# A linear-attention and token-mixer kernel: one hand-given order for all engines, q and k cast by GpSimd's DMAs, states summed on TensorE

## The chip, the core and the metric

The kernel runs on one core of a Trainium2 chip. The core has a matrix engine (TensorE, called PE in the profile, with its weight loads shown apart as PEld), a vector engine (VectorE, DVE), a scalar engine (ScalarE, ACT), a general engine (GpSimd, POOL) and an engine that here only issues DMAs (SyncE, SP). Each of them works through its own instructions in order and waits on semaphores that the others raise. Data comes from and goes to HBM through 16 DMA engines, and any of SP, ACT and POOL may issue a transfer. PE writes to PSUM, which has 8 banks; DVE and ACT bring results from there to SBUF.

The metric is the device time of one execution in microseconds. Three runs of the kernel before gave 156.98 us in the median (156.47 to 158.2).

## The reference

All of q, k and v are [4 batches, 8 heads, 768 positions, 64], in float32. A block-wise linear attention with a decay per head is followed by a mixer over positions:

```python
for b in range(nb):                                  # blocks of 64 positions
    intra = einsum('bhic,bhjc->bhij', qb, kb) * Dmask
    intra = einsum('bhij,bhjd->bhid', intra, vb)
    inter = einsum('bhid,bhde->bhie', qb * lam_pow, kv_state)
    out[:, :, sl] = intra + inter
    kv_state = lam_block * kv_state + einsum('bhsd,bhse->bhde', kb * rev_pow, vb)
x = out.transpose(0, 2, 1, 3).reshape(B, S, H * D)   # [4, 768, 512]
wq, wk = x @ w_q, x @ w_k                            # [4, 768, 64] each
W_tok = einsum('bsd,btd->bst', wq, wk) / sqrt(64)
mixed = einsum('bst,btd->bsd', W_tok, x)
return maximum(mixed, 0) @ w_out                     # [4, 768, 512]
```

Since the decay is a power of the distance, the kernels fold `lam**i` into q and `lam**-j` into v. Then the mask is plain causal, and a state is a plain sum of k-times-v products over all earlier positions.

## The kernel before

The work is cut into 16 pairs: pair n is batch n // 4 and two heads. A pair has six chunks of 128 positions. Its two heads stand in partitions 0 to 63 and 64 to 127.

For each pair, `load` (line 59) issues three DMAs of 384 KB on SP, for q, k and v in float32 (tiles fq, fk, fv). `prepare` then has these steps. POOL casts q and k to bfloat16 (qn line 157, kn line 159) and multiplies v by the decay (vn line 161). PE turns q and k chunk by chunk (trq line 169, trk line 174; six 128-by-128 transposes each). DVE multiplies the turned q by the decay while it brings it from PSUM (qT line 171), and ACT copies the turned k (kT line 176). PE makes the five chunk products of k and v for both heads (dps line 181, ten matmuls), and one DVE scan (gs line 190) adds them up to prefix sums, which are the states.

`attend` works in two halves of three chunks: scores (sc line 212), state times q (oa line 228), mask and cast on DVE (pr line 240), v times masked scores into the same PSUM tile (oa line 246), and the copy to the feature-major result xT on ACT (line 254). `flip` turns xT back to position-major (xp line 260, xnat line 261).

When a batch's four pairs are done, `mixer` runs for it as a generator whose parts are put between the pairs of the next batch: projections (pq line 271, qkT line 278), the turned key side (pk line 281, wkn line 285), py (line 288) and Y (line 292), the mixed result (pm line 298, rmT line 305), and six output tiles (po line 312 on PE, osb line 320 on ACT, and a 256 KB DMA on SP, line 321). The last batch's mixer stands alone at the end.

The order in which the engines get this is set by a scheduler: the code gives the data flow, and the scheduler fills each engine's queue. SP's queue holds the loads and the output DMAs in one line, and each entry can wait. All PSUM tiles come from one pool of 8 banks; staging has 9 buffers for each of fq, fk and fv.

Of the kernel before, what the change touches and what calls it, by code (L numbers as in the profile page):

```python
# [16 lines left out]
CH = 128  # L17
# [4 lines left out]
HALF = 3 * CH  # L22


@with_exitstack
def kernel(
# [28 lines left out]
    def load(b, kk):  # L55
        st = {}
        for nm, src in (("q", q), ("k", k), ("v", v)):
            t = stage.tile([128, 2, NCH, D], F32, tag="f" + nm, name="f" + nm)
            nc.sync.dma_start(  # L59
                out=t,  # L60
                in_=src[b, 2 * kk : 2 * kk + 2].rearrange("h (c p) d -> p h c d", p=128),
            )
            st[nm] = t
        return st
# [4 lines left out]
    staged = {0: load(*pairs[0]), 1: load(*pairs[1])}  # L69


    ident = consts.tile([128, 128], BF16, name="ident")
    make_identity(nc, ident)
    ET = consts.tile([128, S], F32, name="ET")
    nc.gpsimd.iota(
        ET,
        pattern=[[1, S]],
        base=1,
        channel_multiplier=0,
        allow_small_or_imprecise_dtypes=True,  # L80
    )
# [8 lines left out]
    maskc = consts.tile([128, 3, CH], BF16, name="maskc")  # L90
    nc.gpsimd.memset(maskc, 1.0)
    nc.gpsimd.affine_select(
        out=maskc,
        in_=maskc,
        compare_op=ALU.is_ge,
        fill=0.0,
        base=0,
        pattern=[[0, 3], [1, CH]],
        channel_multiplier=-1,
    )  # L100
    coef = consts.tile([128, D, NCH - 1], F32, name="coef")
    nc.vector.memset(coef, 1.0)
    nc.vector.memset(coef[:, :, 0:1], 0.0)

    nc.scalar.preload_act_table_set("natural_log_exp_and_others")
    lnl = consts.tile([128, H], F32, name="lnl")
    nc.scalar.activation(out=lnl, in_=lam_all, func=ACT.Ln)
    lnv = lnl.rearrange("p (k l) -> p k l", l=2)
    lncol = consts.tile([128, NP], F32, name="lncol")
    for hl in range(2):  # L110
        nc.vector.tensor_copy(
            out=lncol[hl * 64 : hl * 64 + 64, :], in_=lnv[hl * 64 : hl * 64 + 64, :, hl]
        )
# [6 lines left out]
    )  # L120
    DvI = consts.tile([128, H, NCH], F32, name="DvI")
# [7 lines left out]
    W = {}  # L129

    def load_weights():
        wqk_f = consts.tile([128, 4, 2 * DHY], F32, name="wqk_f")
# [6 lines left out]
        wqk = consts.tile([128, 4, 2 * DHY], BF16, name="wqk")  # L139
# [4 lines left out]
        wo_f = consts.tile([128, 4, HD], F32, name="wo_f")  # L144
        nc.sync.dma_start(out=wo_f, in_=moe_w_out.rearrange("(kt p) j -> p kt j", p=128))
        wo = consts.tile([128, 4, HD], BF16, name="wo")
        nc.gpsimd.tensor_copy(out=wo, in_=wo_f)
        W["qk"], W["o"] = wqk, wo


    xT, xnat = {}, {}

    def prepare(n):
        b, kk = pairs[n]
        f = staged.pop(n)
        qn = nat.tile([128, NCH, 2, D], BF16, tag="qn", name="qn")
        nc.gpsimd.tensor_copy(out=qn, in_=f["q"].rearrange("p h c d -> p c h d"))  # L157
        kn = nat.tile([128, NCH, 2, D], BF16, tag="kn", name="kn")
        nc.gpsimd.tensor_copy(out=kn, in_=f["k"].rearrange("p h c d -> p c h d"))  # L159
# [3 lines left out]
            in0=f["v"],  # L163
# [3 lines left out]
        trq = pst([128, S], BF16, "trq")  # L167
# [32 lines left out]
    def attend(n, L):  # L200
# [5 lines left out]
        for a in range(2):  # L206
# [15 lines left out]
            for cc in range(3):  # L222
                c = 3 * a + cc
                if c == 0:
                    continue
# [38 lines left out]
    def mixer(b):  # L264
# [44 lines left out]
        for t in range(NCH):  # L309
# [12 lines left out]
            if t % 3 == 2:  # L322
                yield
# [52 lines left out]
```

## Time and profile before

| what | value |
|---|---|
| median of three runs | 156.98 us (156.47 to 158.2) |
| the profiled execution's own time | 157.66 us |
| its span, first to last instruction | 155.9 us |
| PE busy / weight loads / DVE / ACT / POOL | 126.3 / 71.5 / 61.8 / 64.7 / 55.5 us |
| read from HBM / written to it | 20.19 MB / 6.29 MB |
| instructions | 3005 |

The span is the profile's clock: views of the trace count from its start. The profiled execution took 1.76 us more than its span, and was 0.68 us above the median.

A group row names a line of the code, an engine, an operation and its tiles, a count, and then the busy time and the mean of one. Rows of the timeline and of the chain start with the start time and the length in us. Matmuls overlap in PE's pipeline, so a matmul's mean is its latency; how many get through in a time is read from the chain, where each piece counts only until the next one starts.

### The profile page before, as it was taken

The numbers are of one execution on the slowest core, as the hardware profiler recorded it, in microseconds if no ns is written. First come the engines' busy times: TensorE is split into PE (matmuls) and PEld (weight loads), VectorE is DVE, ScalarE is ACT, GpSimd is POOL, SyncE is SP. The second block draws the span as 40 slices with busy tenths as digits, with TensorE's granted clock in tenths as the row PEclk, the third lists the DMA queues.
The fourth block names the chain that finished last, engine by engine and source line by source line (L and its number), as shares of the span: only waits on it lengthen the run. The fifth ranks groups of instructions, "written<-read, shape, count | busy, mean of one in ns | idle before, by whom it ended". The sixth has DMA issues, their size and how long they took to land.

```text
span 155.9 us, 3005 instructions
## 1 busy us (share of the span) xinstructions
PE 126.3 (81%) x1200; PEld 71.5 (46%) x1200; DVE 61.8 (40%) x121; ACT 64.7 (41%) x123; POOL 55.5 (36%) x61
## 2 busy tenths in 40 slices
PE   0234788988899899999498999998298999997890
PEld 0133455646563556465343656554153655543340
DVE  1113536364572286381350458182060647322000
ACT  3831023313122358536222356635204385453881
POOL 5364655475456633003444563004345500000000
PEclk9999999999999999999955699999957999999999
DMA  3999999999999940179999990299999100423055
GB/s 72 222 222 219 218 219 240 293 206 220 209 218 214 226 76 0 69 202 234 307 232 202 228 153 4 81 252 256 279 203 226 24 0 0 169 105 135 0 189 214
DMA packets 79694, 26.67 MB, mean 171 GB/s; under 512 B 76097, under 2 KB 76097, under 8 KB 79681
## 3 DMA queue, kind: packets, MB, share of 16 engines
q1 hardware_dynamic: 79680, 26.49, 79.3%
q8 instruction: 9, 0.15, 0.4%
q14 instruction: 5, 0.03, 0.1%
HBM read 20.19 MB, written 6.29 MB: 170 GB/s over the span
## 4 chain that ended last, share of the span: by engine, by line
PE 47%; SPq 19%; DMA 15%; DVE 6%; issue 5%; POOL 3%; ACT 3%; DVEq 0%; POOLq 0%; ACTq 0%
SPq L59 17%; DMA fv<-in_v_dram 13%; PE po L312 10%; PE oa L246 7%; PE pq L271 6%; PE py L288 5%; PE pm L298 4%; PE oa L228 4%; POOL vn L161 3%; PE xp L260 3%; PE dps L181 3%; DVE pr L240 2%; PE sc L212 2%; PE trq L169 2%; DMA out_dram<-osb 1%
## 5 line engine op out<-in xcount | busy, mean ns | idle before, releaser
L254 ACT CAST xT<-oa 128x384 bf16<-128x384 f32 x32 | 15.3, 479 | 45.9 <-PE oa L246 45.7
L240 DVE TENSOR_TENSOR pr<-sc,maskc 128x384 bf16<-128x384 f32 x64 | 30.8, 544 | 0.0
L161 POOL TENSOR_TENSOR vn<-fv,DvI 128x768 bf16<-128x768 f32 x16 | 23.5, 1472 | 19.7 <-DMA fv<-in_v_dram 14.3
L312 PE MATMUL po<-wo,rmT 128*128 128x512 bf16 x96 | 25.2, 382 | 0.0
L157 POOL CAST qn<-fq 128x768 bf16<-128x768 f32 x16 | 13.2, 823 | 32.2 <-DMA fq<-in_q_dram 31.8
L246 PE MATMUL oa<-pr,vn 128*64 128x128 bf16 x192 | 20.8, 263 | 1.3 <-DVE pr L240 1.3
L261 DVE COPY xnat<-xp 128x768 bf16<-128x768 bf16 x16 | 8.9, 555 | 29.5 <-PE xp L260 29.5
L190 DVE TENSOR_TENSOR_SCAN gs<-coef,dps 128x320 bf16<-128x320 f32 x16 | 13.1, 821 | 17.7 <-PE dps L181 17.4
L176 ACT COPY kT<-trk 128x768 bf16<-128x768 bf16 x16 | 12.9, 807 | 16.8 <-PE trk L174 16.8
L246 PEld LDWEIGHTS <-vn 128*64 128x64 bf16 x192 | 10.6, 124 | 19.1 <-issue 18.1
L228 PE MATMUL oa<-qT,gs 64*64 64x128 bf16 x160 | 18.6, 285 | 0.0
L159 POOL CAST kn<-fk 128x768 bf16<-128x768 f32 x16 | 13.2, 827 | 14.3 <-DMA fk<-in_k_dram 14.3
L169 PE MATMUL trq<-ident,qn 128*128 128x128 bf16 x96 | 10.9, 259 | 7.1 <-POOL qn L157 7.1
L181 PE MATMUL dps<-vn,kn 128*64 128x64 bf16 x160 | 9.4, 286 | 8.3 <-POOL vn L161 8.2
L305 ACT ACTIVATE rmT<-pm 128x384 bf16<-128x384 f32 x32 | 13.4, 510 | 5.4 <-PE pm L298 5.4
L171 DVE TENSOR_TENSOR qT<-trq,dq 128x768 bf16<-128x768 bf16 x16 | 8.9, 554 | 16.6 <-PE trq L169 14.1
L320 ACT COPY osb<-po 128x512 f32<-128x512 f32 x24 | 14.0, 599 | 3.3 <-PE po L312 1.7
L228 PEld LDWEIGHTS <-gs 64*64 64x64 bf16 x160 | 10.6, 158 | 7.5 <-issue 4.7
L260 PE MATMUL xp<-ident,xT 128*128 128x128 bf16 x96 | 10.9, 247 | 2.9 <-ACT xT L254 2.8
L212 PE MATMUL sc<-qT,kT 64*128 64x128 bf16 x192 | 12.9, 250 | 0.0
L174 PE MATMUL trk<-ident,kn 128*128 128x128 bf16 x96 | 10.2, 257 | 3.0 <-POOL kn L159 3.0
L181 PEld LDWEIGHTS <-kn 128*64 128x64 bf16 x160 | 6.9, 149 | 10.3 <-issue 9.2
(37 smaller groups left out, 91.3 us busy)
## 6 DMA issues: line engine op xcount, KB each, us to landing
fq<-in_q_dram SPq DMA_DIRECT2D x16, 384.0 KB, 6.2
fk<-in_k_dram SPq DMA_DIRECT2D x16, 384.0 KB, 6.2
fv<-in_v_dram SPq DMA_DIRECT2D x16, 384.0 KB, 6.3
out_dram<-osb SPq DMA_DIRECT2D x24, 256.0 KB, 2.2
wo_f<-in_moe_w_out_dram SPq DMA_DIRECT2D x1, 1024.0 KB, 7.0
wqk_f<-in_moe_w_q_dram SPq DMA_DIRECT2D x1, 128.0 KB, 6.1
wqk_f<-in_moe_w_k_dram SPq DMA_DIRECT2D x1, 128.0 KB, 4.8
lam_all<-in_lam_dram SPq DMA_DIRECT2D x1, 4.0 KB, 3.4
```

What stands on the lines that cost most here:

```text
L59: nc.sync.dma_start(out=t, in_=src[b, 2 * kk : 2 * kk + 2].rearrange("h (c p) d -> p h c d", p=128),)
L161: nc.gpsimd.tensor_tensor(out=vn, in0=f["v"], in1=DvI[:, 2 * kk : 2 * kk + 2, :].unsqueeze(3).to_broadcast([128, 2, NCH, D]), op=ALU.mult,)
L169: nc.tensor.transpose(trq[:, c * CH : (c + 1) * CH], qn[:, c, :, :], ident)
L181: nc.tensor.matmul(dps[hl * 64 : hl * 64 + 64, :, c], kn[:, c, hl, :], vn[:, hl, c, :], start=True, stop=True, skip_group_check=True,)
L212: nc.tensor.matmul(sc[hl][:, cc, :], kT[r, c * CH : (c + 1) * CH], qT[r, c * CH : (c + 1) * CH], start=True, stop=True, skip_group_check=True,
L228: nc.tensor.matmul(oa[r, cc, :], gs[r, :, c - 1], qT[r, c * CH : (c + 1) * CH], start=first[hl], stop=False, skip_group_check=True,)
L240: nc.vector.tensor_tensor(out=t, in0=sc[hl], in1=maskc, op=ALU.mult)
L246: nc.tensor.matmul(oa[r, cc, :], vn[:, hl, c, :], pr[hl][:, cc, :], start=False, stop=(cc == 2), skip_group_check=True,)
L254: nc.scalar.copy(out=xT[b][:, kk, a * HALF : (a + 1) * HALF], in_=oa)
L260: nc.tensor.transpose(xp[:, t, :], xT[b][:, kk, t * CH : (t + 1) * CH], ident)
L312: nc.tensor.matmul(po, rmT[:, kt, t * CH : (t + 1) * CH], wo[:, kt, :], start=(kt == 0), stop=(kt == 3),)
L320: nc.scalar.copy(out=osb, in_=po)
```

## The change

The tiles and the mathematics stay; what each engine gets, and when, is rewritten.

- **Order.** A manual schedule is switched on: each engine gets its instructions in the order of the code. The code is cut into small functions (`turn`, `states`, `scores`, `inter`, `values`, `flip`, and the mixer's parts) that a loop over the pairs puts in a row. In iteration n PE does the scores of n, transposes of n+1, the flip of n-1, pieces of an earlier batch's mixer, then state times q, v times scores, and the states of n+1.
- **Loads.** v stays on SP in float32. q and k are issued by POOL, with a cast to bfloat16 in the DMA, and no POOL cast is left for them. They run seven pairs ahead (`AHEAD`). q is read two positions at a time (rows of 512 bytes, 768 of them in place of 1536); the order of positions within qT, the scores and the mask changes accordingly, and the copy to xT puts them back.
- **Transposes.** They are made head by head, 24 of 128 by 64 per pair in place of 12 of 128 by 128.
- **States.** Each chunk's product is written to all later states at once, as a matmul whose moving operand repeats v (m times 64 columns, m from 5 to 1) and which adds up in PSUM. A DVE copy takes the place of the scan, and the states lie in one piece for each chunk.
- **Mixer.** Its parts come later: four of a batch's six output tiles are made two batches on; the last batch's end holds four output tiles of the batch before.

The core of the diff:

```diff
+    ctx.enter_context(tc.manual_schedule())
-            nc.sync.dma_start(
-                out=t,
-                in_=src[b, 2 * kk : 2 * kk + 2].rearrange("h (c p) d -> p h c d", p=128),
-            )
+    def load_q(n):
+        t = stage.tile([128, 2, 3, 2 * D], BF16, tag="fq", name="fq")
+        nc.gpsimd.dma_start(
+            out=t,
+            in_=q[b, 2 * kk : 2 * kk + 2].rearrange("h (a p r) d -> p h a (r d)", p=128, r=2),
+        )
+    def load_kv(n):
+        t = stage.tile([128, 2, NCH, D], F32, tag="fv", name="fv")
+        nc.sync.dma_start(
+            out=t, in_=v[b, 2 * kk : 2 * kk + 2].rearrange("h (c p) d -> p h c d", p=128)
+        )
+        t = stage.tile([128, 2, NCH, D], BF16, tag="fk", name="fk")
+        nc.gpsimd.dma_start(
+            out=t, in_=k[b, 2 * kk : 2 * kk + 2].rearrange("h (c p) d -> p h c d", p=128)
+        )
...
-        nc.gpsimd.tensor_copy(out=qn, in_=f["q"].rearrange("p h c d -> p c h d"))
-        nc.gpsimd.tensor_copy(out=kn, in_=f["k"].rearrange("p h c d -> p c h d"))
...
-            nc.tensor.transpose(trq[:, c * CH : (c + 1) * CH], qn[:, c, :, :], ident)
+                    nc.tensor.transpose(
+                        trq[hl * 64 : hl * 64 + 64, a, r, :],
+                        fq[:, hl, a, r * D : (r + 1) * D],
+                        ident,
+                    )
...
-                    vn[:, hl, c, :],
-                    start=True,
-                    stop=True,
+                    vn[:, hl, c, :].unsqueeze(1).to_broadcast([128, m, D]),
+                    start=(c == 0),
+                    stop=(c == NCH - 2),
...
-        nc.vector.tensor_tensor_scan(
+        nc.vector.tensor_copy(out=gs, in_=dps)
...
     for n in range(N):
+        b, kk = pairs[n]
+        if n + AHEAD < N:
+            load_kv(n + AHEAD)
+            load_q(n + AHEAD)
         if n + 2 < N:
-            staged[n + 2] = load(*pairs[n + 2])
+            cast(n + 2)
         if n == 1:
-            load_weights()
+            cast_weights()
+
+        scores(n)
+        if b >= 1 and kk == 1:
+            mix_pk(b - 1)
+        if b >= 1 and kk == 2:
+            mix_pm(b - 1, 0)
+        if b >= 1 and kk == 3:
+            mix_pm(b - 1, 1)
         if n + 1 < N:
-            ready[n + 1] = prepare(n + 1)
-        attend(n, ready.pop(n))
...
+            turn(n + 1)
+        if n >= 1:
+            flip(n - 1)
+        if b >= 1 and kk == 0:
+            mix_pq(b - 1)
+        if b >= 1 and kk == 1:
+            mix_py(b - 1)
+        done = {0: [(2, 2)], 1: [(2, 3)], 2: [(2, 4), (2, 5)], 3: [(1, 0), (1, 1)]}[kk]
+        for back, t in done:
+            if b >= back:
+                mix_po(b - back, t)
+
+        inter(n)
+        values(n)
+        if n + 1 < N:
+            states(n + 1)
+    bl = B - 1
+    flip(N - 1)
+    mix_pq(bl)
+    mix_po(bl - 1, 2)
+    mix_pk(bl)
+    mix_po(bl - 1, 3)
+    mix_py(bl)
+    mix_po(bl - 1, 4)
+    mix_po(bl - 1, 5)
+    mix_pm(bl, 0)
+    mix_pm(bl, 1)
+    for t in range(NCH):
+        mix_po(bl, t)
```

What this does to the queues, at three places. On SP, in the middle of the program before (rows of its queue, in order; a row that stands for several in a row has their count at its end), the loads of a pair stand behind three output DMAs:

```order
L59 DMA fk<-in_k_dram 128x12x64
L59 DMA fv<-in_v_dram 128x12x64
L321 DMA out_dram<-osb 128x512 x3
L59 DMA fq<-in_q_dram 128x12x64
L59 DMA fk<-in_k_dram 128x12x64
L59 DMA fv<-in_v_dram 128x12x64
L321 DMA out_dram<-osb 128x512 x3
```

SP's whole queue after it:

```order
L85 DMA lam_all<-in_lam_dram 128x8
L74 DMA fv<-in_v_dram 128x12x64 x3
L152 DMA wqk_f<-in_moe_w_q_dram 128x4x64
L155 DMA wqk_f<-in_moe_w_k_dram 128x4x64
L158 DMA wo_f<-in_moe_w_out_dram 128x4x512
L74 DMA fv<-in_v_dram 128x12x64 x12
L382 DMA out_dram<-osb 128x512 x2
L74 DMA fv<-in_v_dram 128x12x64
L382 DMA out_dram<-osb 128x512 x22
```

Of the loads only v's last one still stands behind output DMAs. On POOL before, three operations of one pair follow one another:

```order
L157 CAST qn<-fq 128x768
L159 CAST kn<-fk 128x768
L161 TENSOR_TENSOR vn<-fv,DvI 128x768
L157 CAST qn<-fq 128x768
L159 CAST kn<-fk 128x768
```

On POOL after, around the loop's first two iterations, with the semaphores that each waits for (DMASW are those of POOL's own DMAs, DMAHW those of SP's; POOL has eight DMASW and uses them in turn):

```order
L79 DMA fk<-in_k_dram 128x12x64 [waits DMASW6_49]
L65 DMA fq<-in_q_dram 128x6x128 [waits DMASW7_49]
L176 TENSOR_TENSOR vn<-fv,DvI 128x768 [waits DMAHW3_49]
L79 DMA fk<-in_k_dram 128x12x64 [waits DMASW0_49]
L65 DMA fq<-in_q_dram 128x6x128 [waits DMASW1_49]
L176 TENSOR_TENSOR vn<-fv,DvI 128x768 [waits DMAHW7_49,PE_49,Pool_49]
```

A q or k load now waits until the eighth DMA before it on POOL has landed, and the multiplication vn(n+2) stands behind the loads of pair n+7, which wait for those of pair n+3. On DVE, in a later batch, the program before has, from one pair's copies to the next pair's scan:

```order
L261 COPY xnat<-xp 128x6x128
L171 TENSOR_TENSOR qT<-trq,dq_126 128x768
L190 SCALAR_TENSOR_TENSOR gs<-coef,dps 128x320
L240 TENSOR_TENSOR pr<-sc_1140,maskc 128x384
L240 TENSOR_TENSOR pr<-sc_1141,maskc 128x384
L240 TENSOR_TENSOR pr<-sc_1164,maskc 128x384
L240 TENSOR_TENSOR pr<-sc_1165,maskc 128x384
```

and the program after:

```order
L232 CAST gs<-dps 128x320
L257 TENSOR_TENSOR pr<-sc_1166,maskc 128x384
L257 TENSOR_TENSOR pr<-sc_1167,maskc 128x384
L257 TENSOR_TENSOR pr<-sc_1174,maskc 128x384
L257 TENSOR_TENSOR pr<-sc_1175,maskc 128x384
L197 TENSOR_TENSOR qT<-trq,dq_120 128x768
L310 COPY xnat<-xp 128x6x128
```

The four masks now stand ahead of the next pair's qT, and PE has that pair's transposes, the flip and mixer parts between a pair's scores and the matmuls that read the masks.

More of the change, by code (lines that the diff above doesn't have):

```diff
@@ new lines, in mix_po @@
+    def mix_po(b, t):
+        po = pst([128, HD], F32, "po")
+        for kt in range(4):
+            nc.tensor.matmul(
+                po,
+                M[b]["rmT"][:, kt, t * CH : (t + 1) * CH],
+                wo[:, kt, :],
+                start=(kt == 0),
+                stop=(kt == 3),
+            )
+        osb = outp.tile([128, HD], F32, tag="osb", name="osb")
+        nc.scalar.copy(out=osb, in_=po)
+        nc.sync.dma_start(out=out[b, t * CH : (t + 1) * CH, :], in_=osb)
+    build_mask()
@@ L328 @@
+    load_q(1)
+    cast(0)
+    for n in range(2, AHEAD):
+        if n == 3:
+            load_weights()
+        load_kv(n)
+        load_q(n)
+        if n == 2:
+            turn(0)
+            states(0)
+            cast(1)
     for n in range(N):
+        b, kk = pairs[n]
+        if n + AHEAD < N:
+            load_kv(n + AHEAD)
+            load_q(n + AHEAD)
         if n + 2 < N:
[L330 removed]
+            cast(n + 2)
         if n == 1:
[L332 removed]
```

298 lines of the change are left out of this document (151 added, 147 removed).

## The prediction, made before the changed kernel was run

> **What bounds the kernel now.** I read the page first: the engines' busy time, the strips of the DMA and the chain.
>
> ```profile
> PE 126.3 (81%) x1200; PEld 71.5 (46%) x1200; DVE 61.8 (40%) x121; ACT 64.7 (41%) x123; POOL 55.5 (36%) x61
> ...
> DMA  3999999999999940179999990299999100423055
> GB/s 72 222 222 219 218 219 240 293 206 220 209 218 214 226 76 0 69 202 234 307 232 202 228 153 4 81 252 256 279 203 226 24 0 0 169 105 135 0 189 214
> ...
> PE 47%; SPq 19%; DMA 15%; DVE 6%; issue 5%; POOL 3%; ACT 3%; DVEq 0%; POOLq 0%; ACTq 0%
> ```
>
> A slice is 3.9 us. For the first 54 us the DMA is full at about 220 GB/s; then there are three holes. A third of the chain (SPq 19%, DMA 15%) is loads. The queue's own waits, and the timeline of SP (start, length, then what), say why:
>
> ```profile
> SPq L321 <- ACT osb L320: 55.2, 20, 14.2
> ```
>
> ```profile
> 1.23 0.42 SPq L59 DMA_DIRECT2D fq<-in_q_dram  x1
> ...
> 15.82 1.72 SPq L59 DMA_DIRECT2D fq<-in_q_dram  x1
> ...
> 21.16 1.75 SPq L133 DMA_DIRECT2D wqk_f<-in_moe_w_q_dram  x1
> ...
> 31.47 1.69 SPq L59 DMA_DIRECT2D fq<-in_q_dram  x1
> ```
>
> An issue into an empty queue takes 0.42 us, in the full stretch 1.7 us: the transfers then set the pace, 1.73 us for 384 KB, or 5.2 us a pair. And SP stood 55.2 us at output DMAs that waited for ACT, with later loads behind them; those are the holes. So before 54 us the loads bind by rate, and afterwards by the order on SP. What PE does where nothing starves it comes from the chain (start, length until the next piece, what):
>
> ```profile
> 43.73 0.64 PE trk L174 x6
> ...
> 54.41 0.34 PE trk L174 x6
> 54.75 0.42 PE dps L181 x10
> 55.23 0.24 issue
> 55.60 0.33 issue
> 55.93 0.54 DVE pr L240
> ```
>
> The same six transposes take 0.64 us at 43.7 and 0.34 at 54.4. PE ran at about half pace while loads starved it, and that time was hidden behind the loads. Once fed, it pays another 1.1 us a pair (0.24 + 0.33 + 0.54) for masks that its next matmuls need at once. Later in the chain, at full pace, and to the end:
>
> ```profile
> 134.58 0.34 PE xp L260 x6
> 134.91 0.27 PE sc L212 x6
> 135.19 0.29 PE oa L228 x4
> ...
> 135.75 0.37 PE oa L228 x6
> ...
> 138.47 0.28 PE oa L246 x5
> 138.76 1.40 PE po L312 x6
> ...
> 140.49 1.31 PE pq L271 x8
> 141.83 0.49 ACT qkT L278
> 142.36 0.27 PE pk L281 x3
> 142.66 0.37 DVE wkn L285
> 143.07 1.50 PE py L288 x6
> 144.59 0.59 ACT Y L292
> 145.23 1.47 PE pm L298 x8
> ```
>
> ```profile
> 138.79 0.48 ACT L254 CAST xT<-oa 128x384 bf16<-128x384 f32 x1 [0.35 <-PE oa L246]
> ...
> 146.63 5.37 PE L312 MATMUL po<-wo,rmT 128*128 128x512 bf16 x24
> ```
>
> These are the prices of PE's pieces below.
>
> **The change, stage by stage.** The new order gives three stages: A, until the end of iteration 7, in which loads bind; B, iterations 8 to 15, in which PE binds; C, the last batch's mixer.
>
> *Stage A, loads.* By the order, iteration 7 ends with the states of pair 8, whose vn stands on POOL behind the loads of pair 13, which wait until q and k of pair 9 have landed. So ten pairs of q and k, the weights and at least nine v must have come.
>
> - v is unchanged: 1.74 us each. It no longer waits behind q and k, and SP's queue lets it run far ahead, up to all 16. So v takes 9 x 1.74 = 15.7 us to 16 x 1.74 = 27.8 us of DMA time within the stage. If the queues share evenly it is near the upper end, if issue order counts near the lower; I take the middle, 21.7.
> - The weights: from 21.16 to 31.47 SP got through them and one q, k and v; 10.3 less 3 x 1.74 leaves 5.1 us. Of it the two small ones (256 KB in the same short rows as q) are 1.2, so the megabyte of wo in long rows is 3.9, or 1.47 per 384 KB.
> - q in rows twice as long: between 1.47 and 1.74; I take 1.6, the middle.
> - k with a cast in flight: nothing in the trace shows one. It reads the same rows, so 1.74 is nearest; 0.87 if the halved write sets the pace, 3.48 if read and write are each paid.
>
> Ten pairs of q and k are 10 x 3.34 = 33.4. With the first issue at 1.2 and, at the end, two POOL issues at SP's price (0.84) and one vn (1.47, below), A is 1.2 + 33.4 + 5.1 + 21.7 + 2.3 = 63.7 us, between 57.7 and 69.8 by v alone. PE, DVE and ACT work beside it: PE has 3.4 us a pair of its own here (below), even at half pace about what a pair's loads take, and from iteration 4 on some mixer work.
>
> *Stage B, PE.* Per pair, in the new order:
>
> - 24 half-width transposes: 12 full ones cost 0.68. The six sc matmuls, each on half of the array, take 0.27 where six full ones of as many columns take 0.34, so two halves overlap partly. Between 0.68 (two at a time) and 24 x 0.045 = 1.08; I take 0.85.
> - States: 960 columns a head instead of 320, both heads. At 57 ns per 128 columns 0.43 if the heads overlap, 0.86 if not; I take 0.55, near the first, as ten of them with two heads now take 0.42.
> - Scores 0.54. State times q, now from states in one piece: 0.45 (ten at sc's 45 ns) to 0.66 as before; I take 0.5. Values 0.6 (0.67 at the row's 56 ns each). Flip 0.34.
>
> Sum 3.4. A batch's mixer is 1.31 + 2 x 0.27 + 1.50 + 1.47 + 5.37 = 10.2, or 2.55 a pair. That is 5.9 us an iteration. The 1.1 us at the masks goes: 2 us of transposes, flip and po stand between scores and values. Late next is the DMA with 5.1 us a pair, hidden; ACT with 64.7 / 16 = 4.0 and DVE with at most 61.8 / 16 = 3.9 us a pair are hidden too, so the scan's removal earns nothing, nor do POOL's 32 casts. Eight iterations, less the transposes and states (1.4) that the last one has not: 8 x 5.9 - 1.4 = 45.8 us (43 to 52 by the ends above).
>
> *Stage C.* From the last oa row at 138.75 to the end at 155.9 are 17.2 us. Without the six po (1.40) and with four output tiles of the batch before (16 of 24 po, 5.37 x 16 / 24 = 3.6), which cover qkT, wkn and Y (0.49 + 0.37 + 0.59 = 1.45), and 0.5 more for xT's copy, which nothing covers any longer: 18.4 us.
>
> *The sum* is 63.7 + 45.8 + 18.4 = 127.9 of span against 155.9. The profiled execution took 157.66, 1.8 more than its span, and lies 0.7 above the median: 127.9 + 1.8 - 0.7 = 129.0 us.
>
> A rule to weigh against the transposes: the Trainium skill, TensorEngine Tiling (Array Packing), section Feature Incompatibilities, excludes fast weight loading under column tiling. The rows:
>
> ```profile
> L174 PEld LDWEIGHTS <-kn 128*128 128x128 bf16 x96 | 7.7, 118 | 3.9 <-POOL kn L159 3.9
> ...
> L181 PEld LDWEIGHTS <-kn 128*64 128x64 bf16 x160 | 6.9, 149 | 10.3 <-issue 9.2
> ```
>
> ```profile
> 54.68 0.31 PEld L181 LDWEIGHTS <-kn 128*64 128x64 bf16 x10
> ```
>
> A half-width load does take longer, 149 ns against 118. Were they one after another, 24 x 149 ns = 3.6 us instead of 0.85 would add 2.7 us to each iteration of B, and the time would be 129 + 8 x 2.7 = 151. But ten such loads took 0.31 us together, so they overlap; I leave that 1 in 20. By the skill's rule the direction is this rival's, and the trace agrees on the single load and not on the run.
>
> **The rivals.** *POOL's issues are slow (slower).* A POOL issue is in no row. POOL's own work is:
>
> ```profile
> L161 POOL TENSOR_TENSOR vn<-fv,DvI 128x768 bf16<-128x768 f32 x16 | 23.5, 1472 | 19.7 <-DMA fv<-in_v_dram 14.3 <-PE oa L246 2.7 <-PE pk L281 2.0
> L157 POOL CAST qn<-fq 128x768 bf16<-128x768 f32 x16 | 13.2, 823 | 32.2 <-DMA fq<-in_q_dram 31.8 <-PE trq L169 0.4
> ...
> L159 POOL CAST kn<-fk 128x768 bf16<-128x768 f32 x16 | 13.2, 827 | 14.3 <-DMA fk<-in_k_dram 14.3
> ```
>
> Let a pair's two issues hold POOL for X. The vn that iteration 8 needs stands behind 15 pairs of issues, nine vn before it and 5.6 us of constants and weights (55.5 - 23.5 - 13.2 - 13.2): iteration 8 ends at 15 X + 1.2 + 10 x 1.47 + 5.6 = 15 X + 21.5 at the earliest, against 63.7 + 5.9 = 69.6 in my sum. So X counts from 3.2 us on, the time is 129 + 15 (X - 3.2), and it passes 157 at X = 5.1. SP's price gives X = 0.84. If POOL instead handles the 1536 + 768 rows at the pace of its casts, 823 / 768 = 1.07 ns a step, X is 2.5 for one step a row and 4.9 for two. I take 2.5 as nearest, being the same engine; but a loop of several steps a row is not excluded: X = 7 gives 186.
>
> The Trainium skill, DMA: Bandwidth & Descriptors, section Anatomy of one DMA, puts GpSimd's fixed cost at about 2 us a transfer and most of it behind the issue; no run here shows it.
>
> *GpSimd's transfers are moderately slow.* With X between 3.6 and 5, or k at 3.48 (A + 17), the time is 135 to 156; the weight-load rival lies there too.
>
> *The loads come faster.* If k costs 0.87, q 1.47 and v stays in step, A is 1.2 + 23.4 + 5.1 + 15.7 + 2.3 = 47.7; PE then binds iterations 4 to 7 and A is about 54, B 43 at its lower end: 54 + 43 + 18.4 + 1.1 = 117.
>
> *The change does not do what it says.* The queues show the new order, so this is left out.
>
> **How the numbers follow.** My sum with its ends (120 to 135): 0.46. Loads faster (113 to 120): 0.16. Moderately slow (135 to 156): 0.18, with the weight loads' 0.05 in it. Slow issues (above 156): 0.18. Below 113: 0.02. The range 113 to 153 leaves out the slow issues and the ends. About 1% is what a measurement of this kernel can tell from no change: faster by more 0.79, within 0.03, slower 0.18.
>
> **What would show it.** In the profile after: v's loads far ahead and the DMA strip full without holes until about 85 us; POOL's DMA issues as rows on POOL, under 3 us a pair (A right) or above 5 (rival); iteration 8's scores near 64 us; PE pieces in an unbroken row from there, 5.9 us an iteration; trq and trk near 0.43 us for 12 each; the masks ahead of the values that need them; the last 18 us as before with four po between. Wrong would be POOL at the head of the chain, vn waiting on q or k long after v is there, or a DMA strip below 200 GB/s in the first 50 us because the casts are slow.

## The result, and the profile after

The kernel after takes 128.47 us (median of four runs, 128.09 to 129.39); beside it the kernel before took 156.72 us (154.91 to 158.2). The ratio is 0.8238, with a 95% interval of 0.8149 to 0.8327. The profiled execution took 129.39 us, its span is 127.4 against 155.9. Some executions of a kernel, changed or not, are more than 1.5% slower than its fastest; ratios are formed from the others alone, medians from all.

From the page after: busy time, the strips (a slice is now 3.2 us), the chain.

```profile
PE 94.8 (74%) x1382; PEld 63.3 (50%) x1392; DVE 54.8 (43%) x119; ACT 66.9 (53%) x123; POOL 59.3 (47%) x61
...
DMA  2999999999999999999999999998020240424284
GB/s 44 214 166 215 215 308 167 163 164 164 162 163 165 163 164 164 163 165 164 163 163 165 182 237 206 217 219 210 16 87 0 82 153 24 157 86 161 87 331 165
...
PE 54%; POOL 18%; DMA 16%; DVE 4%; issue 4%; ACT 2%; POOLq 0%; ACTq 0%
```

The three holes of the DMA strip are gone: it is full without a break until 86 us (27 of 40 slices) and nearly empty after that. SPq, 19% of the chain before, is not in it any more. In their place stand POOL with 18% and PE with 54%.

The GB/s row must be read with care. It counts what is written (6.29 MB for q and k on POOL's queue, which read twice that), and a casting load writes half of what it reads. One pair is now 768 KB in this row where it was 1152, so 164 GB/s is 4.8 us a pair, as long as one v comes with each q and k (v was somewhat ahead), and the 220 of before were 5.4: about the same pace, not a slower DMA.

The busy time by stage; its columns are the stretch, its length, each engine's busy time (PE, PEld, DVE, ACT, POOL), the granted clock, the DMA share and GB/s. The DMA share adds up the times of all packets, and they overlap, so it can pass 1. The bounds are the first scores, the point where PE takes over the chain (43.35), the scores of iteration 8, and the end of the last values:

```profile
12.20:43.35 31.15, 16.37 (x280) 13.19 (x281) 13.02 (x27) 7.36 (x12) 20.88 (x21) 0.76 1.61 185
43.35:65.18 21.83, 20.91 (x345) 14.93 (x346) 13.50 (x29) 12.66 (x25) 13.85 (x13) 0.87 1.60 164
65.18:108.26 43.08, 40.93 (x654) 27.00 (x662) 26.30 (x57) 29.77 (x57) 13.70 (x11) 1.00 0.89 139
108.26:127.40 19.14, 14.29 (x79) 6.18 (x74) 0.91 (x2) 11.20 (x23) 0.00 (x0) 1.00 0.44 165
```

PE, the first column behind the length, is busy for half of the time until 43.35, and for 95% of it from there to 108.26. So stage A (until 65.18) has two parts. What POOL did in the first is in its timeline (start, length, what, and in brackets how long POOL stood idle before it and for what):

```profile
20.26 1.02 POOL L79 DMA_DIRECT2D fk<-in_k_dram  x1 [2.10 <-DMA fk<-in_k_dram]
23.75 0.82 POOL L65 DMA_DIRECT2D fq<-in_q_dram  x1 [2.48 <-DMA fq<-in_q_dram]
27.35 1.02 POOL L79 DMA_DIRECT2D fk<-in_k_dram  x1 [2.78 <-DMA fk<-in_k_dram]
29.46 0.82 POOL L65 DMA_DIRECT2D fq<-in_q_dram  x1 [1.09 <-DMA fq<-in_q_dram]
30.30 1.48 POOL L176 TENSOR_TENSOR vn<-fv,DvI 128x768 bf16<-128x768 f32 x1
...
59.85 1.07 POOL L79 DMA_DIRECT2D fk<-in_k_dram  x1 [1.49 <-DMA fk<-in_k_dram]
...
62.26 1.49 POOL L176 TENSOR_TENSOR vn<-fv,DvI 128x768 bf16<-128x768 f32 x1
```

The rows begin with the load of pair 6, the first that waits: four issues in a row stand until an earlier load has landed, and the vn of pair 2 stands behind the loads of pairs 6 and 7. The wait is the program's own: each load waits for the eighth DMA before it on POOL. The k of pair 2 landed at 19.98, the q of pair 2 at 23.47, and the k and q of pair 6 were issued 0.28 us later each. The vn of pair 2 is done at 31.78 us, and iteration 2 starts at 32.8, 14.1 us after iteration 1. The last two rows are the load of k of pair 13 and the vn of pair 8, the gate that the prediction named for the end of stage A: it opens at 63.75, when that vn is done.

Two groups of instructions give an issue's price, 1.90 us a pair (columns: total, mean ns, idle before):

```profile
L79 POOL DMA_DIRECT2D fk<-in_k_dram x16 | 17.1, 1071 | 10.9 <-DMA fk<-in_k_dram 9.9
...
L65 POOL DMA_DIRECT2D fq<-in_q_dram x16 | 13.3, 830 | 10.7 <-DMA fq<-in_q_dram 3.6 <-PE trq L191 3.3 <-PE trk L206 2.1
```

The transposes (trq, trk) that the second row names are probably not what q's issues waited for: from pair 10 on each q, too, was issued 0.3 us after the q of four pairs before had landed (pair 10's 0.55 us after).

Stage B is the unbroken row of PE pieces that was expected, with one exception. From the chain (start, length until the next piece, what), iterations 9 and 10 and the start of the last mixer:

```profile
70.28 0.45 PE sc L245 x12
...
71.19 1.48 DVE pr L257 x3
72.67 0.28 DVE wkn L338
...
72.99 1.48 PE py L344 x6
...
76.71 0.44 PE sc L245 x12
77.15 0.65 PE pm L359 x4
77.79 0.49 PE trq L191 x12
78.28 0.34 PE trk L206 x12
78.62 0.44 PE xp L309 x6
...
79.33 1.46 PE po L373 x6
80.79 0.40 PE oa L268 x10
81.18 0.46 PE oa L289 x12
81.64 0.41 PE dps L223 x10
...
108.28 1.04 ACT xT L297 x2
```

In iteration 10 the matmuls that need the masks (L289) come 4 us after the scores, and in this chain PE waits for nothing between them. In iteration 9, the second of its batch, PE still waits for DVE's masks: py needs wkn, and wkn stands behind them on DVE.

### The profile page after: what moved, and what is told of

It reads as the page before. It is cut to its first block, busy times and chain, and to the rows that moved or that the text cites. A ratio compares the mean times of both kernels' runs of the same rounds, so it can differ in the third digit from the quotient of the medians.

```text
span 127.4 us, 3311 instructions
## 1 busy us (share of the span) xinstructions
PE 94.8 (74%) x1382; PEld 63.3 (50%) x1392; DVE 54.8 (43%) x119; ACT 66.9 (53%) x123; POOL 59.3 (47%) x61
## 3 DMA queue, kind: packets, MB, share of 16 engines
q0 software_dynamic: 37376, 6.29, 62.6%
HBM read 20.19 MB, written 6.29 MB: 208 GB/s over the span
## 4 chain that ended last, share of the span: by engine, by line
PE 54%; POOL 18%; DMA 16%; DVE 4%; issue 4%; ACT 2%; POOLq 0%; ACTq 0%
PE po L373 14%; DMA fk<-in_k_dram 14%; POOL fk L79 5%; PE pq L321 5%; POOL vn L176 5%; PE py L344 5%; PE sc L245 4%; PE dps L223 4%; PE oa L289 4%; PE pm L359 4%; POOL fq L65 4%; PE oa L268 4%; PE xp L309 4%; DVE pr L257 4%; PE trq L191 3%
## 5 line engine op out<-in xcount | busy, mean ns | idle before, releaser
L176 POOL TENSOR_TENSOR vn<-fv,DvI 128x768 bf16<-128x768 f32 x16 | 23.7, 1482 | 12.3 <-PE oa L289 8.5
L232 DVE CAST gs<-dps 128x320 bf16<-128x320 f32 x16 | 7.9, 492 | 37.0 <-PE dps L223 37.0
L191 PE MATMUL trq<-ident,fq 128*64 128x128 bf16 x192 | 10.0, 250 | 16.4 <-DMA fq<-in_q_dram 16.4
L79 POOL DMA_DIRECT2D fk<-in_k_dram x16 | 17.1, 1071 | 10.9 <-DMA fk<-in_k_dram 9.9
L65 POOL DMA_DIRECT2D fq<-in_q_dram x16 | 13.3, 830 | 10.7 <-DMA fq<-in_q_dram 3.6
L191 PEld LDWEIGHTS <-fq 128*64 128x64 bf16 x192 | 7.2, 126 | 19.3 <-DMA fq<-in_q_dram 16.9
L223 PE MATMUL dps<-vn,fk 128*64 128x320 bf16 (+4 forms) x160 | 10.7, 269 | 8.1 <-POOL vn L176 8.1
L373 PEld LDWEIGHTS <-rmT 128*128 128x128 bf16 x96 | 8.8, 98 | 10.5 <-issue 1.2
L223 PEld LDWEIGHTS <-fk 128*64 128x64 bf16 x160 | 9.0, 122 | 9.0 <-issue 8.5
L206 PE MATMUL trk<-ident,fk 128*64 128x128 bf16 x192 | 9.9, 248 | 0.0
L289 PE MATMUL oa<-pr,vn 128*64 128x128 bf16 x192 | 9.3, 234 | 0.0
L206 PEld LDWEIGHTS <-fk 128*64 128x64 bf16 x192 | 8.0, 131 | 0.0
## 6 DMA issues: line engine op xcount, KB each, us to landing
fk<-in_k_dram POOLq DMA_DIRECT2D x16, 192.0 KB, 20.2
fq<-in_q_dram POOLq DMA_DIRECT2D x16, 192.0 KB, 20.2
```

What stands on the lines that cost most here:

```text
L65: nc.gpsimd.dma_start(out=t, in_=q[b, 2 * kk : 2 * kk + 2].rearrange("h (a p r) d -> p h a (r d)", p=128, r=2),)
L79: nc.gpsimd.dma_start(out=t, in_=k[b, 2 * kk : 2 * kk + 2].rearrange("h (c p) d -> p h c d", p=128))
L176: nc.gpsimd.tensor_tensor(out=vn, in0=fv, in1=DvI[:, 2 * kk : 2 * kk + 2, :].unsqueeze(3).to_broadcast([128, 2, NCH, D]), op=ALU.mult,)
L191: nc.tensor.transpose(trq[hl * 64 : hl * 64 + 64, a, r, :], fq[:, hl, a, r * D : (r + 1) * D], ident,)
L206: nc.tensor.transpose(trk[hl * 64 : hl * 64 + 64, c * CH : (c + 1) * CH], kn[:, hl, c, :], ident)
L223: nc.tensor.matmul(dps[hl * 64 : hl * 64 + 64, c:, :], kn[:, hl, c, :], vn[:, hl, c, :].unsqueeze(1).to_broadcast([128, m, D]), start=(c = ...
```

## The experiments

Each was timed against the kernel before on the same chip: e1 to e4 on one chip, e5 to e11 on another, e12 on a third. So small differences between two versions are better read from the ratios than from the medians; a difference of ratios is given here in us of the 156.72 of the kernel before. "sc(8)" and "sc(15)" are the starts of the scores of iterations 8 and 15 in the profiled execution.

| run | time, us | ratio to before (95%) | sc(8) | sc(15) | span |
|---|---|---|---|---|---|
| before | 156.72 | 1 | 77.3 | 134.8 | 155.9 |
| after | 128.47 (128.09 to 129.39) | 0.824 (0.815 to 0.833) | 65.1 | 104.2 | 127.4 |
| e1_outs_act | 145.19 (143.83 to 146.27) | 0.921 (0.912 to 0.931) | 72.3 | 120.0 | 142.1 |
| e2_mask_near | 143.2 (141.0 to 144.16) | 0.907 (0.896 to 0.917) | 67.8 | 118.0 | 141.8 |
| e3_all_sp | 136.75 (135.54 to 137.23) | 0.873 (0.866 to 0.880) | 62.2 | 110.5 | 133.5 |
| e4_scan | 131.17 (130.2 to 131.95) | 0.837 (0.829 to 0.844) | 66.0 | 106.6 | 130.2 |
| e5_vn_first | 125.58 (125.53 to 126.06) | 0.809 (0.806 to 0.812) | 59.3 | 100.5 | 123.6 |
| e6_ahead4 | 124.38 (123.89 to 124.65) | 0.800 (0.796 to 0.804) | 60.4 | 99.5 | 122.6 |
| e7_sp_outs_act | 131.41 (129.48 to 132.43) | 0.838 (0.829 to 0.846) | 62.9 | 102.8 | 129.0 |
| e8_pool_slow | 142.96 (142.64 to 144.51) | 0.923 (0.914 to 0.931) | 78.7 | 117.8 | 141.0 |
| e9_comb | 123.93 (123.7 to 124.15) | 0.795 (0.787 to 0.802) | 59.4 | 98.5 | 121.7 |
| e10_v_short | 133.16 (129.82 to 134.5) | none given | 63.9 | 109.3 | 132.5 |
| e11_comb_v_short | 124.2 (123.78 to 125.98) | 0.795 (0.785 to 0.805) | 59.8 | 98.9 | 122.1 |
| e12_comb_pk | 122.97 (121.46 to 124.89) | 0.792 (0.775 to 0.809) | 62.5 | 99.8 | 122.9 |

### Where the 28 us come from

**e1_outs_act**, the kernel before with its output DMAs on ACT, so that no load stands behind them:

```diff
-            nc.sync.dma_start(out=out[b, t * CH : (t + 1) * CH, :], in_=osb)
+            nc.scalar.dma_start(out=out[b, t * CH : (t + 1) * CH, :], in_=osb)
```

> The kernel before, with one thing changed: its 24 output DMAs are issued by ACT instead of SP, so that no load stands behind one. My theory is that half of the gain comes from the order of the queue that the loads stand in: the three holes in the DMA strip close, SP's 55 us behind output DMAs are gone, the loads end near 100 us instead of after 120, and three batches at the old PE price of about 26 us each after the first projection at 47 us, with the old end of 17 us, give 143 us (139 to 147). Rival: the loads' rate alone binds and the holes only fill time that PE needed anyway: 154 to 158 us.

It gained 12.3 us by the ratios (11.5 by the medians). The DMA strip of this kernel is full, but for two dips, until 107 us (30 slices of 3.55 us); that of before broke at 54 and had its last loads near 120:

```profile
DMA  2999999999999999994999999949990002350083
```

**e2_mask_near**, the kernel after with state times q and values right behind the scores, so that masks are needed at once:

```diff
         scores(n)
+        inter(n)
+        values(n)
...
-        inter(n)
-        values(n)
```

> The changed kernel, with state times q and v times scores put right behind the scores again, ahead of the next pair's transposes. Theory: PE then waits for the masks in each iteration, 1.1 us as before or up to 1.5 (two halves), in the 12 iterations that PE binds: 139 to 146 us, and the waits stand in the chain as masks on DVE. Rival: the place of the masks is worth nothing, since the loads or ACT bind there: at most 130 us.

The order is worth 13.0 us by the ratios, 14.7 by the medians. The chain of this kernel, iteration 12, shows the wait that the order removes: 0.10 + 0.36 + 1.49 us between the scores and the values.

```profile
97.26 0.45 PE sc L245 x12
97.71 0.10 DVE pr L257
97.81 0.36 issue
98.17 1.49 DVE pr L257 x3
...
99.70 0.33 PE oa L289 x5
```

That is more than the 1.1 us per pair of before, since DVE now masks all six chunks at once.

**e4_scan**, the kernel after with five separate chunk products and DVE's scan again:

```diff
-                    vn[:, hl, c, :].unsqueeze(1).to_broadcast([128, m, D]),
-                    start=(c == 0),
-                    stop=(c == NCH - 2),
+                    vn[:, hl, c, :],
+                    start=True,
+                    stop=True,
...
-        nc.vector.tensor_copy(out=gs, in_=dps)
+        nc.vector.tensor_tensor_scan(
```

> The changed kernel with the states as before: separate products for each chunk, and the scan on DVE, with the states strided. Theory: PE's product of states and q goes back from 0.40 to 0.66 us, the products stay at 0.41, and DVE has 0.33 us more a pair that is hidden: 12 iterations of 0.26 us, so 130.5 to 132.5 us. Rival: the scan delays the masks behind it on DVE, and PE waits for it too: 134 us or more. A second rival: the states' form is worth nothing, within 0.7 us of the changed kernel.

With the scan the kernel takes 2.0 us longer by the ratios, 2.7 by the medians. The scan's row, and iteration 10 in the chain:

```profile
L234 DVE TENSOR_TENSOR_SCAN gs<-coef,dps 128x320 bf16<-128x320 f32 x16 | 13.1, 821 | 35.0 <-PE dps L225 35.0
```

```profile
76.63 0.52 PE oa L277 x10
...
77.60 0.28 PE dps L225 x10
77.88 0.44 PE sc L254 x12
78.32 0.34 PE pm L368 x2
...
78.66 0.54 DVE pr L266
...
79.25 0.53 PE trq L194 x12
```

In PE's own pieces nothing is lost: the products are 0.13 us cheaper (0.28 against 0.41) and the strided states 0.12 dearer (0.52 against 0.40). But the scan is 0.33 us longer than the copy (821 against 492 ns) and stands ahead of the masks on DVE. Here the transposes start 1.37 us after the scores, right behind the end of the first mask; in the kernel after they started 1.08 us after them (77.79 - 76.71), right behind pm. A mask frees a PSUM tile, and all 8 banks are shared, so a late mask is felt by work that does not read it. That reading of the wait is inferred. The runs do not overlap those of the kernel after (130.2 to 131.95 against 128.09 to 129.39), but the intervals of the ratios do, a little. The time lies in the theory's range, but not for its reason, dearer products on PE. The rival's reason, masks behind the scan, fits the chain; its price (134 us or more) was too high.

By the ratios the three are 12.3 + 13.0 + 2.0 = 27.3 of the 27.6 us gained (by the medians 11.5 + 14.7 + 2.7 = 28.9 of 28.2). Each was measured from its own kernel, e1 from the one before and the others from the one after, so they need not add up: the sum makes a further large part unlikely and does not exclude it. The half-width transposes and the mixer's later parts were not tried alone.

### Whether the casting DMAs matter

**e3_all_sp**: q, k and v in float32 on SP, casts on POOL, the order kept.

```diff
-        t = stage.tile([128, 2, NCH, D], BF16, tag="fk", name="fk")
-        nc.gpsimd.dma_start(
+        t = stage.tile([128, 2, NCH, D], F32, tag="fk", name="fk")
+        nc.sync.dma_start(
...
+        nc.gpsimd.tensor_copy(out=kn, in_=fk)
```

> The changed kernel with q and k loaded by SP in float32 in the order v, k, q of each pair, and cast by POOL as before (0.82 us each); order and transposes as in the changed kernel. Theory: the casting DMAs bring nothing; they let v run ahead of what is needed and put vn behind waits for later pairs. With one queue in step, nine pairs at 3 x 1.73 us less the long rows of q, and the weights, are there at 53 us, the last states of iteration 7 come near 56 instead of 65 us, and the time is 119 to 121 us. Rival: casting in the DMA shortens the loads or frees POOL: 128.5 us or more.

A miss: 136.75 us. The loads were in fact earlier, sc(8) at 62.2 instead of 65.1. But the output DMAs now stood behind the loads on SP, and the loads were themselves held up there by the transfers before them. ACT, with four output buffers, waited, and PE behind it: iteration 11 took 13.9 us. From the waits (total, times, longest):

```profile
ACT osb L384 <- DMA out_dram<-osb: 11.8, 4, 9.5
```

**e7_sp_outs_act**: the same with the output DMAs on ACT.

```diff
-        nc.sync.dma_start(out=out[b, t * CH : (t + 1) * CH, :], in_=osb)
+        nc.scalar.dma_start(out=out[b, t * CH : (t + 1) * CH, :], in_=osb)
```

> All loads in float32 on SP and casts on POOL as in the run before that put all loads on SP, but the output DMAs on ACT. There the loads came earlier (iteration 8 began at 62.2 instead of 65.1 us), and then ACT stood 9.5 us at output tiles whose DMAs waited on SP behind loads. Theory: without that wait iteration 8 begins near 61 us and the rest is as in the changed kernel, 43 + 19 + 1.9: 123 to 126 us. Rival: with q and k in float32 on the way the loads still bind in iterations 8 to 12, and it stays at 130 us or more.

Also a miss, and a helpful one. The time is in the rival's range, but the rival's reason, loads that bind in iterations 8 to 12, is not what the trace shows. sc(8) is at 62.9 and stage B runs at the pace of the kernel after (39.9 us from sc(8) to sc(15), against 39.1). The loss is in the last mixer: from sc(15) to the end 26.2 us instead of 23.2, for ACT issues each output itself:

```profile
121.02 0.59 ACT osb L384
...
121.64 0.34 ACTq L385
...
122.07 0.59 ACT osb L384
```

An output tile takes ACT 1.05 us (0.34 of it the issue, ACTq), and the end now waits for ACT.

So float32 loads on SP give a stage A between that of the kernel after (65.1) and that of the best order with casting loads (59.3 in e5_vn_first, below). What the change gets from POOL's DMAs is mostly not a faster transfer: outputs stand behind a third of the loads instead of all, at no cost to ACT.

### What POOL's place in the chain costs

**e8_pool_slow**: three needless casts of 768 columns on POOL for each pair from pair 2 on, which raises X, the time that a pair's issues hold POOL, from 1.9 to 4.4 us.

```diff
+        if n >= 2:
+            for _ in range(3):
+                nc.gpsimd.tensor_copy(out=scr, in_=ET)
```

> The changed kernel with three extra POOL casts of 768 columns (2.46 us) behind each pair's two DMA issues from pair 2 on, to raise what a pair's issues hold POOL from the measured 1.9 us to 4.4. By the prediction's formula iteration 8 ends at 15 x 1.9 + 21.5 + 13 x 2.46 = 82 us at the earliest instead of 70: 140 us (136 to 144). Rival one: POOL is already on the path, and all 32 us show: 155 us or more. Rival two: POOL's time is hidden wholly: 128 to 130 us.

142.96 us. The formula of the prediction's rival (iteration 8 ends at 15 X + 21.5; here 15 x 1.9 + 13 x 2.5 + 21.5 = 82.5) gave a time of 140, and iteration 8 ended at 83.8. Neither rival came: all of POOL's added work (155 us or more) or none of it (130 or less). POOL is at the head of the chain:

```profile
POOL 48%; PE 40%; DVE 3%; issue 2%; ACT 2%; DMA 2%; POOLq 0%; ACTq 0%
```

**e5_vn_first**: vn of pair n+2 ahead of the loads of pair n+7 on POOL.

```diff
     for n in range(N):
         b, kk = pairs[n]
+        if n + 2 < N:
+            cast(n + 2)
         if n + AHEAD < N:
             load_kv(n + AHEAD)
             load_q(n + AHEAD)
-        if n + 2 < N:
-            cast(n + 2)
```

> The changed kernel with vn(n+2) ahead of the loads of pair n+7 on POOL, so that vn no longer stands behind the wait for pair n+3. Theory: in the first 43 us PE waits for vn, and vn for later pairs' landings (32.0 us for k of pair 4) and then for the weights' casts; without the first of these waits iterations 3 and 7 end 3 to 8 us earlier: 121 to 126 us. Rival: vn is late because the data itself is late, or because PE binds from 43 us on whatever the start: 127.5 to 129.5 us. If the loads are issued later behind vn's own waits, it is slower than 129.5.

2.9 us faster than the kernel after (2.3 by the ratios), and sc(8) at 59.3. Iteration 2 starts at 26.2 instead of 32.8. Of the 5.8 us by which iteration 8 starts earlier, 2.1 are lost again by iteration 15 (41.2 us from sc(8) to sc(15) against 39.1): in the chain the transposes of pair 13 wait for its q until 83.97. The chain now belongs to the loads:

```profile
DMA 51%; PE 24%; POOL 16%; issue 3%; ACT 2%; DVE 1%; POOLq 0%; ACTq 0%
```

**e6_ahead4**: loads four pairs ahead instead of seven, so that vn no longer waits for an issue that waits for a landing.

```diff
-AHEAD = 7
+AHEAD = 4
```

> The changed kernel with loads four pairs ahead instead of seven. Then v cannot run far ahead, and vn(n+2) no longer waits for the landing of pair n+3. Theory (v running ahead and the waits cost stage A): iteration 8 starts near 57 instead of 65 us, 120 to 124 us in all. Rival: it is the depth that keeps the DMA full; with four pairs the strip shows holes and v waits behind output DMAs: 129.5 us or more.

4.1 us faster than the kernel after (3.7 by the ratios), though sc(8) came at 60.4, later than the 57 expected. Fewer loads ahead are better here: sc(8) is 1.1 us later than in e5, but nothing is lost behind it (39.1 us from sc(8) to sc(15)). In this trace no issue on POOL waits for a landing between 9 and 50 us.

**e9_comb**, both edits at once (the two diffs above).

> The kernel after with both earlier edits at once: vn of iteration n+2 ahead of the loads on POOL, and q, k, v loaded four iterations ahead instead of seven. Theory (what is left before iteration 8 is the rate of the transfers, which both edits already reach): the scores of iteration 8 start at 58 to 60 us, where either edit alone had 59.3 and 60.4, and the time is 122 to 125 us. Rival (the two waits were different ones and add up, 2.9 and 4.1 us): iteration 8 at 56 us or earlier, 121 us or less.

123.93 us, sc(8) at 59.4, as the theory had it: the waits did not add up. Two ways of taking away the same wait lead to the same floor, 59.3 to 60.4 us. What sets that floor was not separated; the chains of e5 and of this run name loads.

**e10_v_short**, the kernel after with four buffers for v:

```diff
+    vst = ctx.enter_context(tc.tile_pool(name="vst", bufs=4))
...
-        t = stage.tile([128, 2, NCH, D], F32, tag="fv", name="fv")
+        t = vst.tile([128, 2, NCH, D], F32, tag="fv", name="fv")
```

> The kernel after with four buffers for v instead of nine, so that the load of v for pair n+4 waits for vn of pair n; nothing else is changed. Theory (the prediction's term for v that runs ahead: every v that lands before it is needed takes 1.74 us of transfer time from q and k): one or two v fewer until the scores of iteration 8, which start at 62 to 64 us instead of 65.1; 125.5 to 127.5 us. Rival 1 (POOL's waits and PE set stage A, not the amount loaded): 128 to 129 us. Rival 2 (v becomes late, since a v takes 14.4 us to land): iteration 8 at 67 us or later, above 130 us.

Half right. sc(8) came at 63.9, inside the 62 to 64 of the theory. But all four runs are slower than the slowest of the kernel after, by 0.4 to 5.1 us. The profiled execution is the slowest of the four (134.5 us), so the size of what follows holds for it alone. SP's timeline says why:

```profile
53.15 16.83 SPq L75 DMA_DIRECT2D fv<-in_v_dram  x4
70.03 6.00 SPq L383 DMA_DIRECT2D out_dram<-osb  x2
76.13 0.39 SPq L75 DMA_DIRECT2D fv<-in_v_dram  x1
76.56 15.65 SPq L383 DMA_DIRECT2D out_dram<-osb  x6
```

Loads of v that waited for a buffer were still being issued at 70 us, where SP had got through all but the last at 63.4 in the kernel after (11.45 + 51.92):

```profile
11.45 51.92 SPq L74 DMA_DIRECT2D fv<-in_v_dram  x12
```

The output DMAs stood behind them, ACT waited 3.82 us for an output buffer, and PE nearly stood still from 81 to 84 us (0.56 us busy) and then ran at half pace until 91, at a granted clock of 0.51. It is the fault of the kernel before turned round, outputs behind loads, as in e3.

**e11_comb_v_short**, four buffers for v on top of e9_comb (the two diffs above).

> Both edits of the run before (vn first, four iterations ahead) and four buffers for v. Theory (with the two waits gone, stage A is set by how much has to be loaded, so that fewer v ahead help here even if they do not in the kernel after): the scores of iteration 8 at 55 to 58 us, 119 to 122 us. Rival (v becomes late, or v's run-ahead took nothing from q and k): 123.5 us or more.

124.2 us, like e9_comb. It says nothing on v's run-ahead: in both kernels SP issued twelve v by 45 us and the other four after 59, since four pairs ahead already limits v.

**e12_comb_pk**, e9_comb with pk ahead of the scores:

```diff
-        scores(n)
         if b >= 1 and kk == 1:
             mix_pk(b - 1)
+        scores(n)
```

> The kernel of e9_comb with pk (and so its copy wkn on DVE) ahead of scores(n) instead of behind it, in the second iteration of each batch. Theory (wkn stands on DVE behind four masks of 0.55 us, and py on PE waits for it; that is what is left of the waits at the masks): py of iterations 9 and 13 starts some 0.7 us earlier, each of them takes 5.7 us where the others take 5.1 to 5.3 and these took 6.5, and the time falls by 1.5 us, to 122 to 123 us. Rival (the masks themselves, which the same iteration's values need, become the wait in its place): iterations 9 and 13 stay at 6.3 us or more and the time at 123.5 to 124.5.

The step behaves as expected: py follows the flip without a wait, and iterations 9 and 13 take 5.4 us instead of 6.4. From the chain, iteration 13:

```profile
88.98 0.19 PE pk L334 x3
...
89.23 0.36 PE sc L245 x11
...
90.39 0.44 PE xp L309 x6
90.83 1.41 PE py L344 x6
```

The time is 122.97 us, but its interval of 0.775 to 0.809 overlaps that of e9_comb. The profiled execution was the slowest of the six (124.89 us), with sc(8) 3.1 us later than in e9_comb; from sc(8) to sc(15) it took 37.3 us against 39.1. So the saving in stage B is shown in the trace, and in the time it is only likely. With e5_vn_first, e6_ahead4, e9_comb and e11_comb_v_short it is among the versions that beat both kernels of this study.

## Why the prediction came out right

129.0 us were predicted, 128.47 measured; of the span, 127.9 against 127.4. The three stages: 63.7, 45.8 and 18.4 predicted; 65.2, 43.1 and 19.1 measured. The errors of +1.5, -2.7 and +0.7 nearly cancel, so it is luck that the total is closer than its parts.

- **Loads behind outputs.** Right as to place: SP's share of the chain is gone and the strip is full until 86 us. e1_outs_act gives its size, 12.3 us by the ratios.
- **Stage A's gate.** Right as to place and time: the vn of pair 8 stands behind the loads of pair 13, and was done at 63.75. But it is not what ended the stage. PE reaches the same place 1.0 us later: the values of iteration 7 (L289) end at 64.76. From 43.35 on it is PE that the chain names, and part of this is at half pace (eight pq matmuls 2.19 us at 47.29, 1.30 at 66.85; the granted clock is 0.50 from 42.2 to 49.0). PE was late there because it had waited for vn before 43.35.
- **"Loads bind" in stage A.** Too simple: this reading put POOL's order down to the loads' rate. e5, e6, e9 and e11 start the scores of iteration 8 at 59.3 to 60.4, with every load in the same form. The other 5 to 6 us come from vn standing behind issues that wait for landings, some of them probably by way of PE's half pace (in e5 the clock is at half for 3.4 us from 38.1, not for 6.8 from 42.2). The prediction's sum had the gate right and called its price a rate, so its 63.7 for stage A is in part luck.
- **Its signs of being wrong.** Two of the three appeared, though the time was right. The strip was below 200 GB/s (164), but that sign was ill chosen, since the row counts what is written. And vn did wait on q and k long after v was there: the v of pair 2 landed at 13.4 us, its vn began at 30.30. This was the real one, and e5 shows its price.
- **v's 21.7 us.** SP issued the twelfth v at 45.5 us and it landed at 61.1; the thirteenth landed at 64.5. So twelve had come when the gate opened, and 21.7 is 12.5 times 1.74. The middle between two ends was a guess, and a good one. e10 (sc(8) 1.2 us earlier) agrees in direction, while what it did to SP spoils its time.
- **k at 1.74, q at 1.6.** All 16 pairs by these prices are 1.2 + 5.1 + 16 x (1.74 + 1.74 + 1.6) = 87.6 us; the strip was full until about 86. With the other two prices for k, 0.87 and 3.48, it would have been full until 74 or 115.
- **POOL's issues.** X was taken as 2.5, and is 1.90: 1.07 for k and 0.83 for q. That is neither SP's 0.42 nor one step a row (k would be twice q). It is below the 3.2 from which it counts, so the slow rival fell. e8 shows that its mechanism was real and its formula close at X = 4.4; the threshold itself was not tried. The Trainium skill, DMA: Bandwidth & Descriptors, Anatomy of one DMA, puts most of its fixed 2 us behind the issue, at the landing. These rows show the issue alone, 0.83 to 1.07 us; what follows it cannot be told here from the transfers ahead in the queue (20.2 us to landing in the median).
- **Stage B's pieces.** All a little dear. Transposes 0.46 + 0.34 = 0.80 (0.85 taken), states 0.41 (0.55), scores 0.44 (0.54), state times q 0.40 (0.5), values 0.46 (0.6), only the flip dearer, 0.44 (0.34). The sum is 2.95 instead of 3.4: twelve half-width matmuls run in the time of six full ones (trk, 0.34) up to that of eight (sc, 0.44). An iteration took 39.1 / 7 = 5.6 us instead of 5.9.
- **"The 1.1 us at the masks goes."** Mostly. In one iteration of four a wait stays, through wkn on DVE: 6.4 us each for iterations 9 and 13 where their neighbours take 5.1 to 5.4. e12 takes it away.
- **"The scan's removal earns nothing."** Wrong, by 2.0 to 2.7 us in e4 (by ratios and by medians). The prediction argued from DVE's busy time, 3.9 us a pair. That busy time is no bound, but the scan stands ahead of the masks, and the moment at which the masks come is one.
- **The mixer at the end.** 19.1 instead of 18.4: the term for xT's copy was 0.5, and PE waits for both copies, 1.04 us (592 ns each instead of 479; these copies now also put the positions back).
- **The rule on column tiling.** The Trainium skill, TensorEngine Tiling (Array Packing), Feature Incompatibilities, excludes fast weight loading under column tiling. The prediction's rival put its price at 2.7 us an iteration. By the rows 24 half-width transposes take 0.80 us, and twelve (trk, 0.34) just what six full ones took before. No run here shows the loss.
- **The rivals.** Faster loads (117) did not come: the pace of a pair stayed near 5 us. Its floor for stage A, 54, is below the 59.3 that even e5 reached.

## What to carry to other kernels

Ask of each entry of a queue which other entries it makes wait: here loads behind outputs (12.3 us), outputs behind loads (e3, e10), and arithmetic behind waiting issues on POOL (2.3 to 3.7 us by the ratios) were the same fault in three places, and a longer run-ahead made the last one worse.

An engine at 40% busy is not hidden if the next matmul waits for its one instruction: put independent matmuls between scores and masked values (13.0 us), and price what stands ahead of the mask in its queue.

Where an experiment misses as e3 did, keep the part that arrived on time (sc(8) at 62.2) apart from the part that broke, and undo the break alone.

## What the runs showed of the hardware that was not expected

- An issue of a strided load on POOL takes 1.07 us for 1536 rows and 0.83 for 768, so by these two points most of it does not depend on the rows. That is 2.0 to 2.6 times SP's 0.42.
- A transfer that casts to half the size is hardly faster: 768 KB written per pair at 164 GB/s take 4.8 us (one v to each q and k); e3's float32 loads, with the same long rows of q, took SP 5.1 us a pair (from the issue of one v at 45.58 us to that of the sixth after it at 76.23).
- A full DMA held back the two queues in different ways. POOL issued the loads of six pairs without a wait; the next four issues each waited for an earlier landing (2.10, 2.48, 2.78, 1.09 us), a wait that the program sets. On SP the issue itself grew longer: 1.7 us each in the full stretch before the change, 4.3 us in the mean for the twelve v of the kernel after, against 0.42 at the start.
- While PE is starved at first, its pieces run at half pace in all these kernels (trk 0.64 against 0.34 us). Where the trace has a record of the granted clock, clock and pace agree: in the kernel after it is 0.50 from 21.7 to 35.4 and from 42.2 to 49.0 us, with trk at 0.64 at 45.90, and 1.00 later, with 0.34 at 57.79. The kernel before reads 1.00 between 40 and 50 us although its pieces run at half pace. But its record of the clock begins only at 50.9 us, with a step to full, and a view prints 1.00 where there is no record: that 1.00 is no measurement.
